# Norm passes moved from VectorE to GpSimd, and urgent work put first, in a two-layer attention and MLP kernel

## The chip, the cores and the metric

The kernel runs on one core of a Trainium2 chip. A core has TensorE (PE, matrix products), VectorE (DVE), ScalarE (ACT, here mostly exponentials), GpSimd (POOL) and SyncE (SP, which only starts transfers). They run side by side and wait for one another by semaphores. The metric is device time in microseconds (us) from the first to the last instruction; lower is better. "Faster" or "slower" by over 2% is told apart from "the same".

## The reference

Two layers, each an attention block A and an MLP block B, over 2048 tokens of width 512. Attention has 32 heads of width 16 that share one set of keys and values. B mixes shifted tokens and then applies an MLP of width 1792. The norms have no learned factors.

```python
def _layernorm(x):  return (x - mean(x)) / sqrt(var(x) + 1e-5)

def _A_ref(x, wq, wk, wv, wo):                 # x: 1 x 2048 x 512
    q = (x @ wq) as 32 heads of 16;  k = x @ wk;  v = x @ wv     # k, v: one head for all
    p = softmax(q k^T * 16**-0.5)              # 32 x 2048 x 2048
    return (p v) @ wo

def _B_ref(x, w1, w2, w3, w4):
    h = gelu(layernorm(x) @ w1)
    g = the four quarters of h, shifted by +1, -1, +2, -2 tokens
    x1 = x + g @ w2
    return x1 + gelu(layernorm(x1) @ w3) @ w4

x = x + _A_ref(layernorm(x));  x = x + _B_ref(layernorm(x))      # layer 0
x = x + _A_ref(layernorm(x));  x = x + _B_ref(layernorm(x))      # layer 1
```

Two facts shape the kernel. 32 x 2048 x 2048 exponentials per layer have to be made. And layer 1's attention needs keys of all tokens, so it cannot finish a query before layer 0 has finished its last token.

## The kernel before

The Python program builds a list of operations with durations it assumes, and runs a list scheduler over them (class `Plan`). The order that comes out is the instruction order of each engine; semaphores guard the data. So a changed duration, engine or priority changes the order of everything after it. Tokens come in tiles of 128, grouped in chunks: 4 x 4 tiles in layer 0, and 4, 4, 4, 2, 2 tiles in layer 1. While one chunk's attention runs, the dense work of the chunk before it (output projection, mixer, MLP) fills TensorE.

**Exponentials.** Most of them go through ScalarE, two score banks of 512 columns at a time (`declare_unit`). Seven EA buffers hold the results until the value product (PV) has read them:

```python
o = q.feeds = op("ACT", lambda e: e.activation(self.EA[:, ea, :, :], self.PB[:, b0:b0 + 2, :], ACTF.Exp,
                                               scale=0.25), writes=bk + [("EA", ea)], ...)     # L994
```

The others are made as a "pair" on VectorE and GpSimd (`declare_pair`): VectorE turns scores into 16-bit integers J (L1015), which are bit patterns of powers of two; two shifted copies JK (L1025) are made on GpSimd, or on VectorE if four are outstanding there; three value products with weighted values VD add them up. The pair is given out (`assign`) only if banks are free and if VectorE has little side work ready:

```python
if self.pl.backlog() > y or ...:  return False         # y = 1 (us) in most chunks
```

**Priorities.** Small numbers go first: 0 for scores of ScalarE's units, 2 for value products, 10 for dense work (`URGE`: 1.0 for the last chunk of layer 0). One rule lets dense work follow dense work, ahead of all else, to save a switch on TensorE:

```python
if stick and o.prio > 2 and o.pe[0] == self.pe_kind and not any(... > x for x in due):
    key = (self.STICK, o.seq)                          # STICK = -1
```

When TensorE has done little for a while, the plan inserts products of ones by zeros (`filler`: ONES, NIL) that keep its clock up.

**Norms.** Each norm has statistics (`stats`, L723 and L725), the power -0.5 (`rstd`, on GpSimd, L745) and one pass per tile (`apply`, L752). In the mixer there are two norms in a row: block B's input is itself a norm, and B begins with a norm; the second factor follows from the first variance, so one pass more per tile (L1289) does it:

```python
def apply(self, out, src, tb, tags, writes, dur, prio):
    self.pl.op("DVE", lambda e: e.tensor_scalar(out=out, in0=src, scalar1=self.MV[:, tb, 0:1],
               scalar2=self.SM[:, 0, tb:tb + 1], op0=ALU.subtract, op1=ALU.mult), ...)            # L752
...
# mixer_in: Y = norm(X); ZR = norm(Y)
for tb in tiles:
    self.apply(self.Y[:, tb % 6, :], self.X32[:, tb, :], tb, ...)
    op("DVE", lambda e, tb=tb: e.tensor_scalar(out=self.ZR[:, tb % 4, :], in0=self.Y[:, tb % 6, :],
               scalar1=self.SM[:, 1, tb:tb + 1], scalar2=0.0, op0=ALU.mult, op1=ALU.add), ...)    # L1289
```

The rows ZR (four tiles) are transposed on TensorE (L769), copied back (L776) and fed to the products with W1 or W3. The same four slots of ZR serve the mixer's second norm, the MLP's norm, and the input norms of both layers (`ln_in`; in layer 1 its rows give the keys and values of layer 1).

**The end of a block.** When all keys of a block of heads are done, `block_end` copies the sum (ACCF), makes reciprocals of the row sums and scales (OS, OT) at priority 5; after the eighth block the chunk's output projection and the rest follow (`chunk_end`).

Of the kernel before, what the change touches and what calls it, by code (L numbers as in the profile page):

```python
# [31 lines left out]
class Plan:  # L32
# [29 lines left out]
    SPARE = 0  # L62

    def __init__(self, nc, pool_banks):
        self.nc = nc
        self.res = {}
        self.ops = []
        self.now = 0.0
        self.free_at = {e: 0.0 for e in ENGINES}
        self.heap = {e: [] for e in ENGINES}  # L70
        self.order = {e: [] for e in ENGINES}
        self.events = [0.0]
        self.pool = [(0.0, b) for b in pool_banks]
        self.pool_last = {}
        self.left = 0
        self.dma_free = 0.0
        self.pe_kind = None
        self.pe_end = 0.0
        self.lane = [0.0] * 4
        self.port = 0.0  # L80
        self.window = 0
        self.activity = [0.0]
        self.warm = False
        self.release = 0.0
        self.entry = 0.0
        self.pace = None
        self.filler = None
        self.debt = 0.0
        self.debt_at = 0.0
        self.base = 10.0  # L90
        self.units = []
        self.attach = None
        self.loose = False
# [97 lines left out]
    def _pick(self, eng, t, dense=False):  # L191
        h = self.heap[eng]
        if dense:
# [6 lines left out]
            and self.pe_kind == "P"  # L200
        due = list(limit) + self.due(h, t) if stick else ()
        best = None
        bank = None
        for o in h:
            if o.ready > t + 1e-9:
                continue
# [12 lines left out]
            if stick and o.prio > 2 and o.pe[0] == self.pe_kind and not any(self.run_end(o, t) + self.SWITCH > x for x in due):  # L219
                key = (self.STICK, o.seq)  # L220
            if best is not None and key > best[0]:
                continue
# [269 lines left out]
EPS = 1e-5  # L492
# [3 lines left out]
class Kernel:  # L496
# [4 lines left out]
    URGE = ((10, 10, 10, 1.0), (10, 10, 10, 1.5, 10))  # L501
    SPILLED = 7
    SHIFTS = (1, -1, 2, -2)
# [47 lines left out]
    def memory(self):  # L551
# [32 lines left out]
        self.EA = sb("EA", [self.N_EA, 2, 512])  # L584
        self.J = sb("J", [self.N_J, 1024], dt.uint16)
# [134 lines left out]
    def stats(self, src, tiles, tagf, prio):  # L720
        op = self.pl.op
        for tb in tiles:
            op("DVE", lambda e, tb=tb: e.bn_stats(self.ST6[:, tb, :], src(tb)),  # L723
               reads=[tagf(tb)], writes=[("ST", tb)], dur=0.606, prio=prio)
            op("DVE", lambda e, tb=tb: e.bn_aggr(self.MV[:, tb, :], self.ST6[:, tb, :]),  # L725
               reads=[("ST", tb)], writes=[("MV", tb)], dur=0.09, prio=prio)

    def rstd(self, tiles, prio, both=False):
        op = self.pl.op
        a, b = tiles[0], tiles[-1] + 1  # L730
        mv = self.MV[:, a:b, 1]
        k = 2 if both else 1

        def tg(name):
            return [(name, t) for t in tiles]
        var, aux = self.SM[:, 2, a:b], self.SM[:, 3, a:b]
        op("DVE", lambda e: e.tensor_scalar(out=var, in0=mv, scalar1=EPS, scalar2=None, op0=ALU.add),  # L737
           reads=tg("MV"), writes=tg("S2"), dur=0.08, prio=prio, port=True)
        if both:
            op("DVE", lambda e: e.reciprocal(aux, var), reads=tg("S2"), writes=tg("S3"), dur=0.1, prio=prio)  # L740
            op("DVE", lambda e: e.tensor_tensor(out=aux, in0=aux, in1=mv, op=ALU.mult),
               reads=tg("MV"), writes=tg("S3"), dur=0.08, prio=prio, port=True)
            op("DVE", lambda e: e.tensor_scalar(out=aux, in0=aux, scalar1=EPS, scalar2=None, op0=ALU.add),
               writes=tg("S3"), dur=0.08, prio=prio, port=True)
        op("POOL", lambda e: e.tensor_tensor(out=self.SM[:, 0:k, a:b], in0=self.SM[:, 2:2 + k, a:b],  # L745
                                             in1=self.MH[:, 0:k, a:b], op=ALU.pow),
           reads=tg("S2") + (tg("S3") if both else []) + [("MH",)], writes=tg("R1") + (tg("R2") if both else []),
           dur=0.3 + 0.2 * (b - a) * k, prio=self.QUICK if prio is None else prio)

    def apply(self, out, src, tb, tags, writes, dur, prio):  # L750

        self.pl.op("DVE", lambda e: e.tensor_scalar(  # L752
            out=out, in0=src, scalar1=self.MV[:, tb, 0:1], scalar2=self.SM[:, 0, tb:tb + 1],
            op0=ALU.subtract, op1=ALU.mult),
            reads=tags + [("MV", tb), ("R1", tb)], writes=writes, dur=dur, prio=prio, port=True)

    def transpose(self, tiles, dst, dtags, prio):

        op = self.pl.op
        n = len(tiles)  # L760
        for hd in range(2):
            L = Late()
            for j in range(2):
                dc = 2 * hd + j

                def fpe(e, dc=dc, j=j, L=L):
                    ins = None
                    for i, tb in enumerate(tiles):
                        ins = e.transpose(self.PBH[:, L.bank, j * 512 + i * 128:j * 512 + (i + 1) * 128],  # L769
                                          self.ZR[:, tb % 4, dc * 128:(dc + 1) * 128], self.IDENT)  # L770
                    return ins
                op("PE", fpe, reads=[("ZR", tb % 4) for tb in tiles] + [("ID",)], writes=[L],
# [8 lines left out]
    def ln_in(self, la, tiles, prio=None):  # L781
# [5 lines left out]
        self.rstd(tiles, prio)  # L787
        for tb in tiles:
            self.apply(self.ZR[:, tb % 4, :], src(tb), tb, [("X", tb)], [("ZR", tb % 4)],
                       0.456 if la else 0.355, prio)  # L790
# [3 lines left out]
                       [[("YT", slot, hd, t % 4) for t in tiles] for hd in range(2)], prio)  # L794
# [286 lines left out]
    def block_end(self, la, c, b, end):  # L1081
# [22 lines left out]
        else:  # L1104
            self.last_copy = op("DVE", lambda e: e.tensor_copy(acc, self.PB[:, self.ACC, 0:n]),
               writes=[("AC",), ("ACCF", m)], dur=t_ps(n), prio=0, side=False)
        L = Late()
# [7 lines left out]
        op("PE", fz, reads=[("ACCF", m), ("SELC",)], writes=[L], pe=("F", 60 * nq, 4 * nq), prio=5, take=L)  # L1115
# [4 lines left out]
        op("DVE", frec, writes=[L, ("RZ", m)], dur=0.17, prio=5, give=L)  # L1120
        M = Late()
        for h in range(nq // 2):
# [8 lines left out]
            op("PE", fx, reads=[("RZ", m), ("ID",)], writes=[M], pe=("P", 256, 256, range(4)), prio=5,  # L1131
# [3 lines left out]
           reads=[("ACCF", m)], writes=[M, ("OS", m)], dur=t_ps(n), prio=5, give=M)  # L1135
        r0 = 64 * (b % 2)
        hw = n // 2
        if c == len(self.CHUNKS[la]) - 1 and b >= self.LATE_OT:
            N = Late()

            def fo(e):
# [9 lines left out]
               pe=("P", 2 * hw, hw, (r0 // 32, r0 // 32 + 1)), prio=5, take=N)  # L1151
            op("DVE", lambda e: e.tensor_copy(self.OT[r0:r0 + 64, b // 2, 0:n], self.PB[r0:r0 + 64, N.bank, 0:n]),
               writes=[N, ("OT", b)], dur=t_ps(n), prio=5, give=N)
        else:
# [4 lines left out]
               reads=[("OS", m)], writes=[("OT", b)], dma=128 * n, parts=8, prio=5)  # L1159
# [9 lines left out]
    def pump(self, now):  # L1169
# [3 lines left out]
        while True:  # L1173
            if sum(1 for o in self.units[-4:] if not (o.placed and o.end <= now + 1e-9)) >= 3:
                break
            while self.hi in self.given:
                self.hi += 1
            if self.hi >= n:
                break
# [103 lines left out]
    def mixer_in(self, la, c, tiles, tail, more=None):  # L1283
# [3 lines left out]
        for tb in tiles:  # L1287
            self.apply(self.Y[:, tb % 6, :], self.X32[:, tb, :], tb, [("X", tb)], [("Y", tb % 6)], 0.456, None)
            op("DVE", lambda e, tb=tb: e.tensor_scalar(  # L1289
# [3 lines left out]
               dur=0.265, port=True)  # L1293
# [71 lines left out]
    def mlp(self, la, tiles, tail, defer=False):  # L1365
# [14 lines left out]
        for f in range(14):  # L1380
# [10 lines left out]
            if tail:  # L1391
                op("ACT", lambda e, f=f, L=L: e.activation(self.G2[:, f, 0:n], self.PB[:, L.bank, 0:n],
                                                           ACTF.Gelu_apprx_tanh),
                   writes=[L, ("G2", f)], dur=0.0505 + n / 1200, give=L)
# [18 lines left out]
        self.mlp_out(la, tiles)  # L1413

    def mlp_out(self, la, tiles):
        op = self.pl.op
        g2 = [("G2", f) for f in range(14)]
        for i, tb in enumerate(tiles):
            L = Late()
            for h in range(7):  # L1420
                def fpe(e, h=h, i=i, tb=tb, L=L):
                    ins = None
                    for f in (2 * h, 2 * h + 1):
                        ins = self.dot(e, L.bank, 512, self.G2[:, f, i * 128:(i + 1) * 128], self.W4[:, f, :],
# [50 lines left out]
```

## Time and profile before

| | before |
|---|---|
| device time, median of 3 runs | 1617.7 us (1616.78 to 1618.05) |
| span of the profiled run | 1615.1 us |
| exponentials on ScalarE (1024 columns, mean) | 1504, 1105 ns |
| conversions to J on VectorE (512 columns) | 1088, so 544 pairs |
| shifts JK on GpSimd / on VectorE | 983 (1054 ns) / 105 (702 ns) |
| norm passes on VectorE | 32 Y<-X 934 ns, 32 ZR<-Y 733 ns, 16 + 16 ZR<-X 904 and 524 ns, 32 second passes 539 ns |
| start of steady exponentials / end of the last | 43.8 us / 1549.3 us |
| mean granted TensorE clock | 0.999 |

How to read the lines: L12 is a line of the kernel's program; `out<-in` names the tiles; `x` is a count. In a group the numbers after the bar are busy us and mean ns of one, then the idle time of that engine just before, and what released it. Waits are "who waited for whom: total us, times, longest us". Timeline lines are start us, length us, engine, line, operation and count, with the idle time before in brackets. The busy time of one instruction on ScalarE overlaps the next: steady exponentials follow each other every 0.917 us (246 in 225.69 us). W3, W4, W1, W2 and WO products all stand under L612, and `W` in a tile's name is one of the weights, `G` the MLP's inner values, `GP` the mixer's, `ZT` transposed norm rows.

### The profile page before, as it was taken

To read this page: it belongs to the slowest core of one execution; us is meant where nothing else is said; L and a number is where in the kernel's file an instruction comes from. 1 tells how busy PE (TensorE), PEld (TensorE's weight loads), DVE (VectorE), ACT (ScalarE), POOL (GpSimd) and SP (SyncE) were. 2 spreads that over 40 slices of the span, in tenths; PEclk is the share of its full clock that TensorE was granted. 3 is DMA by queue.
4 is the path that set the end of the run, shared out by engine and by line. 5 is a ranking of instruction groups with operands and counts; after the bars stand their busy time and mean duration, and the time that the engine had idled before them with its cause. 6 is when DMAs were issued, how large, how long until landed. Compare 5 with 4: busy or idle time off the path is not lost.

```text
span 1615.1 us, 63788 instructions
## 1 busy us (share of the span) xinstructions
PE 1567.6 (97%) x28953; PEld 654.9 (41%) x28953; DVE 1245.5 (77%) x2222; ACT 1500.5 (93%) x1580; POOL 1118.4 (69%) x1083
## 2 busy tenths in 40 slices
PE   8999999999999999999999999999999999999999
PEld 3333333434333333333333434333343334544555
DVE  8777887778887679887776678878678885778863
ACT  4999999999999999999998499999999998999952
POOL 4798877866787766776673477677777867768631
PEclk9999999999999999999999999999999999999999
DMA  6100010001000001000000000100000000000000
GB/s 207 17 6 5 7 18 6 6 4 17 7 6 4 6 4 19 6 4 2 2 2 2 3 9 9 19 4 5 9 18 5 6 5 15 16 8 7 6 17 19
DMA packets 32144, 21.55 MB, mean 13 GB/s; under 512 B 12672, under 2 KB 31360, under 8 KB 31872
## 3 DMA queue, kind: packets, MB, share of 16 engines
q1 hardware_dynamic: 31872, 17.47, 4.5%
q8 instruction: 226, 3.70, 1.0%
q14 instruction: 46, 0.38, 0.1%
HBM read 7.90 MB, written 2.10 MB: 6 GB/s over the span
## 4 chain that ended last, share of the span: by engine, by line
ACT 64%; PE 33%; DVE 2%; issue 0%; DMA 0%; POOL 0%; SPq 0%; POOLq 0%
ACT EA L994 59%; PE PB L612 12%; PE PB L950 10%; PE PB L1073 8%; ACT G L1403 2%; PE PB L769 1%; ACT L994 1%; ACT GP L1323 1%; ACT L1403 1%; ACT L1323 0%; DVE ZR L752 0%; DVE ST L723 0%; DMA X<-in_A_x_dram 0%; DVE J L1015 0%; PE PB L878 0%
## 5 line engine op out<-in xcount | busy, mean ns | idle before, releaser
L994 ACT ACTIVATE EA<-PB 128x1024 bf16<-128x1024 f32 x1504 | 1390.6, 1105 | 66.6 <-PE PB L1073 33.8
L1025 POOL TENSOR_SCALAR JK<-J 128x1024 uint16<-128x1024 uint16 x983 | 1035.6, 1054 | 402.4 <-DVE J L1015 257.4
L1015 DVE TENSOR_SCALAR J<-PB 128x512 uint16<-128x512 f32 x1088 | 702.4, 683 | 185.1 <-PE PB L950 181.1
L950 PE MATMUL PB<-QT,KT 32*128 32x512 bf16 (+1 forms) x4608 | 624.4, 359 | 30.5 <-ACT EA L994 18.6
L1073 PE MATMUL PB<-EA,VP 128*32 128x256 bf16 (+1 forms) x6784 | 388.4, 265 | 0.5
L950 PEld LDWEIGHTS PB<-QT,KT 32*128 32x128 bf16 x4608 | 161.3, 91 | 448.0 <-ACT EA L994 351.4
L1073 PE MATMUL PB<-JK,VD 128*32 128x256 bf16 (+1 forms) x4864 | 291.3, 265 | 2.9 <-POOL JK L1025 1.9
L1073 PEld LDWEIGHTS PB<-EA,VP 128*32 128x32 bf16 x6784 | 157.1, 95 | 175.3 <-issue 149.6
L612 PE MATMUL PB<-ONES,NIL 128*32 128x512 bf16 x1984 | 177.1, 387 | 7.4 <-DVE ZR L752 2.8
L1073 PEld LDWEIGHTS PB<-JK,VD 128*32 128x32 bf16 x4864 | 114.9, 95 | 128.0 <-issue 78.8
L612 PE MATMUL PB<-ZT,W 128*32 128x512 bf16 (+2 forms) x2816 | 166.6, 341 | 0.0
L1073 PE MATMUL PB<-J,VD 128*32 128x256 bf16 (+1 forms) x2432 | 154.9, 264 | 1.3 <-DVE J L1015 0.8
L612 PE MATMUL PB<-W,G 128*32 128x512 bf16 x1792 | 122.9, 380 | 0.3 <-DVE X L1279 0.3
L1396 DVE CAST G<-PB 128x512 bf16<-128x512 f32 (+2 forms) x126 | 72.3, 582 | 34.7 <-PE PB L612 33.4
L612 PEld LDWEIGHTS PB<-ZT,W 128*32 128x32 bf16 x2816 | 67.7, 96 | 26.1 <-issue 13.0
L1025 DVE TENSOR_SCALAR JK<-J 128x1024 uint16<-128x1024 uint16 x105 | 73.2, 702 | 2.9 <-PE PB L1073 1.9
L1073 PEld LDWEIGHTS PB<-J,VD 128*32 128x32 bf16 x2432 | 60.6, 95 | 35.4 <-issue 21.6
L612 PEld LDWEIGHTS PB<-ONES,NIL 128*32 128x32 bf16 x1984 | 49.6, 96 | 42.4 <-issue 11.2
L745 POOL TENSOR_TENSOR SM<-SM,MH 128x4 f32<-128x4 f32 (+4 forms) x30 | 31.7, 1058 | 40.8 <-DVE SM L737 24.8
L1133 DVE TENSOR_TENSOR OS<-ACCF,PB 128x512 bf16<-128x512 bf16 (+1 forms) x72 | 44.6, 622 | 17.7 <-PE PB L1127 17.3
L612 PEld LDWEIGHTS PB<-W,G 128*32 128x32 bf16 x1792 | 42.2, 96 | 31.8 <-issue 11.7
L1403 ACT ACTIVATE G<-G 128x3584 bf16<-128x3584 bf16 (+2 forms) x18 | 46.0, 2601 | 9.4 <-DVE G L1396 9.3
(88 smaller groups left out, 861.5 us busy)
## 6 DMA issues: line engine op xcount, KB each, us to landing
OT<-OS SPq DMA_DIRECT2D x424, 8.0 KB, 1.8
W<-in_B_w_dram SPq DMA_DIRECT2D x2, 1792.0 KB, 14.4
QT<-QS SPq DMA_DIRECT2D x40, 64.0 KB, 2.4
X<-in_A_x_dram SPq DMA_DIRECT2D x8, 256.0 KB, 5.4
out_dram<-OUTB SPq DMA_DIRECT2D x16, 128.0 KB, 1.7
OT<-OS SPq DMA_DIRECT2D x104, 4.0 KB, 1.7
W<-in_B_w_dram SPq DMA_DIRECT2D x2, 512.0 KB, 8.4
WQ<-in_A_wq_dram SPq DMA_DIRECT2D x1, 512.0 KB, 5.0
```

The lines of the kernel that those rows point to most:

```text
L612: ins = e.matmul(self.PB[32 * g:32 * g + 32, bank, 0:n], lhsT=lhsT[:, 32 * g:32 * g + 32], rhs=rhs, start=start, stop=stop, tile_position= ...
L745: op("POOL", lambda e: e.tensor_tensor(out=self.SM[:, 0:k, a:b], in0=self.SM[:, 2:2 + k, a:b], in1=self.MH[:, 0:k, a:b], op=ALU.pow), read ...
L769: ins = e.transpose(self.PBH[:, L.bank, j * 512 + i * 128:j * 512 + (i + 1) * 128], self.ZR[:, tb % 4, dc * 128:(dc + 1) * 128], self.IDENT)
L950: ins = e.matmul(self.PB[:, bank, j * n:(j + 1) * n], lhsT=self.KT[32 * h:32 * h + 32, la, (kb + j) * 128:(kb + j + 1) * 128], rhs=self.QT ...
L994: o = q.feeds = op("ACT", lambda e: e.activation(self.EA[:, ea, :, :], self.PB[:, b0:b0 + 2, :], ACTF.Exp, scale=0.25), writes=bk + [("EA" ...
L1015: o = op("DVE", lambda e, i=i, L=L: e.tensor_scalar(out=J[:, i * 512:(i + 1) * 512], in0=self.PB[:, L.bank, :], scalar1=128 * LOG2E * 0.25 ...
L1025: x = op(eng, lambda e, k=k, r=r: e.tensor_scalar(out=self.JK[:, r, :], in0=J, scalar1=float(self.STEPS[k]), scalar2=1.0, op0=ALU.add, op1 ...
L1073: ins = e.matmul(self.PB[32 * x:32 * x + 32, self.ACC, p * hw:p * hw + hw], lhsT=v[:, la, kb + j, :], rhs=ap[:, i, j * w + u * hw:j * w + ...
L1133: op("DVE", lambda e: e.tensor_tensor(out=self.OS[:, m, 0:n], in0=acc, in1=self.PB[:, M.bank, 0:n], op=ALU.mult), reads=[("ACCF", m)], wri ...
L1323: return e.activation(self.GP[:, par, :, 2:2 + n], self.GP[:, par, :, 2:2 + n], ACTF.Gelu_apprx_tanh)
L1396: op("DVE", lambda e, f=f, L=L: e.tensor_copy(self.G2[:, f, 0:n], self.PB[:, L.bank, 0:n]), writes=[L, ("G2", f)], dur=t_ps(n), give=L)
L1403: ins = e.activation(self.G2[:, a:a + 7, 0:n], self.G2[:, a:a + 7, 0:n], ACTF.Gelu_apprx_tanh)
```

## The change

It moves the norm passes and most small statistics to GpSimd (not those at the start of layer 0), raises the priority of the aggregation of statistics on VectorE, and splits the two powers into two instructions, so that the first norm need not wait for the second's factor. Layer 1's input norm gets rows of its own: QS, which otherwise holds query projections. Value products that one of the next three exponentials waits for go first (PINNED). The rule that dense work follows dense work is off while an urgent dense operation (priority up to 1.2) is ready, and near the end. In the last chunk of each layer the end of a block gets priority 1.0, and in the last chunk of layer 1 all that follows has it too. In the last chunk the MLP's gelu writes into the EA buffers, which are free by then, and not into G2, which the products before it still read.

```diff
+    PINNED = -2
+    RUSHED = 1.2
 ...
         stick = eng == "PE" and not dense and not joins and self.STICK is not None and t < self.pe_end + 0.05 \
-            and self.pe_kind == "P"
+            and self.pe_kind == "P" \
+            and not any((0 < o.prio <= self.RUSHED if o.side else self.closing) and o.ready <= t + 1e-9 for o in h)
+        pinned = {p for u in self.units[-3:] if not u.placed for p in u.preds
+                  if p.eng == "PE" and p.prio == 2 and not p.placed} if eng == "PE" and not dense else ()
 ...
+            if eng == "ACT" and self.closing and o.side and not all(u.placed for u in self.units[-4:]):
+                continue
 ...
+            if o in pinned:
+                key = (self.PINNED, o.seq)
 ...
-    URGE = ((10, 10, 10, 1.0), (10, 10, 10, 1.5, 10))
+    URGE = ((10, 10, 10, 1.0), (10, 10, 10, 1.5, 1.0))
+    RUSH = ((10, 10, 10, 1.0), (10, 10, 10, 5, 1.0))
+    CLOSING = 12
 ...
+        self.G2E = self.EA.rearrange("p a b c -> p (a b) c")
 ...   # stats
-               reads=[("ST", tb)], writes=[("MV", tb)], dur=0.09, prio=prio)
+               reads=[("ST", tb)], writes=[("MV", tb)], dur=0.09, prio=self.QUICK if prio is None else prio)
 ...   # rstd: var + eps, power, and for both norms the second factor
+        eng = "DVE" if early else "POOL"
+        def power(out, src, tags, r):
+            op("POOL", lambda e: e.tensor_tensor(out=out, in0=src, in1=self.MH[:, 0, a:b], op=ALU.pow),
+               reads=tags + [("MH",)], writes=tg(r), dur=0.3 + 0.2 * (b - a), prio=prio)
-        op("DVE", lambda e: e.tensor_scalar(out=var, in0=mv, scalar1=EPS, scalar2=None, op0=ALU.add),
+        op(eng, lambda e: e.tensor_scalar(out=var, in0=mv, scalar1=EPS, scalar2=None, op0=ALU.add),
            reads=tg("MV"), writes=tg("S2"), dur=0.08, prio=prio, port=True)
+        power(one, var, tg("S2"), "R1")
         if both:
-            op("DVE", lambda e: e.reciprocal(aux, var), ...)
-            op("DVE", ... aux * mv);  op("DVE", ... aux + EPS)
+            op(eng, lambda e: e.tensor_tensor(out=aux, in0=one, in1=one, op=ALU.mult), ...)
+            op(eng, ... aux * mv);  op(eng, ... aux + EPS)
+            power(two, aux, tg("S3"), "R2")
-        op("POOL", ... both powers in one tensor_tensor)
 ...   # apply
-        self.pl.op("DVE", lambda e: e.tensor_scalar(
+        early = prio is not None
+        self.pl.op("DVE" if early else "POOL", lambda e: e.tensor_scalar(
 ...
-            reads=tags + [("MV", tb), ("R1", tb)], writes=writes, dur=dur, prio=prio, port=True)
+            reads=tags + [("MV", tb), ("R1", tb)], writes=writes, dur=dur if early else 0.65, prio=prio if early else self.QUICK, port=True)
 ...   # ln_in
+        base = (self.QS, "QS") if la else (self.ZR, "ZR")
         for tb in tiles:
-            self.apply(self.ZR[:, tb % 4, :], src(tb), tb, [("X", tb)], [("ZR", tb % 4)],
+            self.apply(base[0][:, tb % 4, :], src(tb), tb, [("X", tb)], [(base[1], tb % 4)],
 ...   # block_end: all its side operations take prio=fin in place of 5
+        fin = min(5, self.RUSH[la][c])
 ...   # pump
+            self.pl.closing = self.hi + self.CLOSING >= n
 ...   # mixer_in, second pass
-            op("DVE", lambda e, tb=tb: e.tensor_scalar(
+            op("POOL", lambda e, tb=tb: e.tensor_scalar(
 ...
-               dur=0.265, port=True)
+               dur=0.65, prio=self.QUICK, port=True)
 ...   # mlp and mlp_out, last chunk
-                op("ACT", lambda e, f=f, L=L: e.activation(self.G2[:, f, 0:n], self.PB[:, L.bank, 0:n],
+                op("ACT", lambda e, f=f, L=L: e.activation(self.G2E[:, f, 0:n], self.PB[:, L.bank, 0:n],
                                                            ACTF.Gelu_apprx_tanh),
-                   writes=[L, ("G2", f)], dur=0.0505 + n / 1200, give=L)
+                   writes=[L, ("EA", f // 2)], dur=0.0505 + n / 1200, give=L)
```

## What was predicted

> **What bounds the kernel now.** I read the totals of the page first, then the chain that ended last, then ScalarE's waits and its timeline at each gap, and last the other engines' timelines at those moments.
>
> The page's busy totals, and its chain by engine:
>
> ```profile
> PE 1567.6 (97%) x28953; PEld 654.9 (41%) x28953; DVE 1245.5 (77%) x2222; ACT 1500.5 (93%) x1580; POOL 1118.4 (69%) x1083
> ...
> ACT 64%; PE 33%; DVE 2%; issue 0%; DMA 0%; POOL 0%; SPq 0%; POOLq 0%
> ```
>
> ScalarE and TensorE are both close to full. TensorE's 97% holds 1984 matmuls of ones by zeros (`ONES,NIL`), which keep its clock up. The timeline shows 112 dense matmuls in 6.22 us, so four side by side take 0.222 us, and 1984/4 x 0.222 = 110 us of TensorE is spare in the whole run. VectorE and GpSimd have a quarter of their time free, and the chain gives them 2% and 0%: a change of their load alone cannot be worth its own size. ScalarE's waits (total us, times, longest us):
>
> ```profile
> ACT EA L994 <- PE PB L1073: 33.8, 18, 10.2
> ACT EA L994 <- PE PB L950: 31.8, 12, 18.3
> ACT GP L1312 <- PE PB L612: 14.0, 1, 14.0
> ACT G L1392 <- PE PB L612: 11.1, 14, 6.5
> ACT G L1403 <- DVE G L1396: 9.3, 1, 9.3
> ```
>
> Row 1: an exponential waits for the value product (L1073) that still reads the EA buffer it is to write. Row 2: it waits for scores; 21.8 us of it lie in the first 80 us, which this change leaves alone, and 8.4 us at 930 us, where layer 1 waits for its last keys. Rows 3 to 5 are the end, after the last exponential (1549.3 us). The longest wait of row 1 in ScalarE's and TensorE's timelines:
>
> ```profile
> 898.57 1.02 ACT L994 ACTIVATE EA<-PB 128x1024 bf16<-128x1024 f32 x1 [10.15 <-PE PB L1073]
> 889.11 4.93 PE L612 MATMUL PB<-W,G 128*32 128x512 bf16 x88
> 893.87 1.05 PE L612 MATMUL PB<-ZT,W 128*32 128x256 bf16 x32
> 895.07 1.48 PE L612 MATMUL PB<-ZT,W 128*32 128x256 bf16 x48
> ```
>
> TensorE is not idle there. It runs 10 us of dense MLP products while the value product that would free EA stands ready: the plan's STICK rule lets dense work follow dense work. The same shape is at 1369 us (5.2 us) and 1181 us (3.1 us). By stretch, row 1 has 20.9 us between 855 and 931, and 10.6 us between 1100 and 1400.
>
> The second norm at the end of layer 0, in VectorE's timeline:
>
> ```profile
> 767.36 3.35 DVE L752 TENSOR_SCALAR Y<-X,MV,SM 128x512 bf16<-128x512 f32 x4
> 784.82 0.34 DVE L1289 TENSOR_SCALAR ZR<-Y,SM 128x512 bf16<-128x512 bf16 x1
> 812.09 1.12 DVE L1289 TENSOR_SCALAR ZR<-Y,SM 128x512 bf16<-128x512 bf16 x3 [1.33 <-PE PB L769]
> ```
>
> The mixer's second norm writes the four row slots of ZR. The first norm (Y) is done at 770.7, but ZR is filled only at 813.2: one slot at 785, the other three when layer 1's input norm of the chunk before (L752, ZR<-X, until 807) and its transposes (until 811) are done with the same slots. So 42 us of the path to layer 1's last keys are a buffer wait. I found it by asking why work that was ready at 771 came at 812.
>
> **What the Trainium skill says.** (1) "SBUF — State Buffer", Who interferes with whom: a `tensor_scalar` of VectorE in a two-port mode and a GpSimd instruction exclude each other for the whole instruction. The trace agrees (min/median/max ns):
>
> ```profile
> L752 DVE TENSOR_SCALAR Y<-X,MV,SM x32: 529/1048/1403, 230.8 to 1560.5; 128x512 bf16<-128x512 f32 x32
> L1289 DVE TENSOR_SCALAR ZR<-Y,SM x32: 256/346/1134, 233.0 to 1561.9; 128x512 bf16<-128x512 bf16 x32
> ```
>
> The same instruction takes 529 ns or over 1 us; the surplus is up to half a microsecond and more, which fits a wait for a GpSimd shift of 1054 ns. (2) "GPSIMD Engine Reference", Engine selection: one-input elementwise work is about as fast on GpSimd as one element a cycle, two-input work some 2x slower. The trace agrees: the 1024-element shift (one input) took 1054 ns, the 512-element add of Y and X (two inputs) 1169 ns. (3) "Perfetto Trace Analysis", Optimizing Scalar/DVE Operations: moving work between these two might not help, since they share a port; no run shows this yet. (4) The same page, Identifying the Most-Contended Engine: matmul busy time is a bad measure of headroom. It agrees: 177.1 us of the busy sum are the ones-by-zeros matmuls.
>
> **The change, part by part.**
>
> *Norm passes to GpSimd.* Off VectorE go, by the groups of lines: 28.9 (32 Y<-X) + 23.0 (32 ZR<-Y) + 14.0 (16 ZR<-X of layer 1) + 16.8 (32 second scalings) = 82.7 us, with some 15 us of small statistics (the means and variances proper stay, and their last step now goes first on VectorE). On GpSimd, half of a 1054 ns shift is 0.53 us, and the plan is told 0.65, so I take 0.6: 112 x 0.6 = 67 us. Nine second powers add about 9 x 0.4 us (two of 1.02 us in place of one of 1.64), and 26 + 27 small operations about 0.15 us each = 8 us. GpSimd goes from 1118 to some 1197 us (74%) and does not become the bound. What VectorE gains buys something in one way only: the plan hands a pair of exponentials to VectorE and GpSimd only when no more than 1 us of side work stands ready on VectorE. The nine mixer groups, ten MLP groups and seven input norms hold it by their passes for something like 30 to 45 us (half of the 82.7, the rest being port waits). At 36 to 38 pairs per 100 us (75 shifts in 400 to 500) that is 11 to 17 pairs; some are lost as GpSimd's bursts push shifts back to VectorE. I take 7 pairs more, each an exponential of 0.917 us less on ScalarE (225.69 us for 246): **-6 us**.
>
> *Urgent value products (PINNED).* A value product that one of the next exponentials waits for goes ahead of all. The 10.6 us at 1181 and 1369 vanish; the displaced dense products move into stretches where TensorE runs ones by zeros (152 of them in 1400 to 1500, 38 fours, 8.4 us). Most of it is gained: **-8 us**. The 20.9 us at 855 to 931 count with the boundary.
>
> *Boundary (own rows in QS, RUSH, urgency over STICK).* The 42 us buffer wait goes, so W1, gelu, mixing, W3 and W4 of layer 0's last chunk start earlier. Yet ScalarE loses only 20.9 + 8.4 = 29.3 us there, and TensorE has little room: from 750 to 1055 it ran 28 + 220 + 160 ones-by-zeros matmuls, 102 fours x 0.222 = 22.6 us, and was idle some 5. So at most 27 us can be pressed out, and that only with perfect packing. GpSimd's passes lengthen the last norm before the keys: now four take 1.92 us (924.41), then 4 x 0.6 = 2.4. I take somewhat under half: **-12 us**.
>
> *Tail (URGE and RUSH 1.0 for the last chunk, CLOSING, gelu into EA).* From 1549.3 to the end TensorE is almost solid with W3 and W4 of the last two chunks; only what is not dense can go:
>
> ```profile
> L612 PE MATMUL PB<-ONES,NIL 128*32 128x512 bf16 x116 | 9.5, 384 | 2.2 <-DVE MV L725 0.7 <-DVE ZR L752 0.7 <-DVE OS L1133 0.5
> ```
>
> 116/4 x 0.222 = 6.4 us plus 2.2 idle = 8.6. With the last chunk first, the chunk before fills its waits; GpSimd's slower norms (three passes 1.8 instead of 1.06 us, the mixer's chain about 1 us longer) then lie beside dense work. **-6 us**.
>
> Sum: -6 - 8 - 12 - 6 = -32 us. The parts overlap, since they draw on the same spare TensorE time (110 us, much of it where ScalarE is the limit and nothing dense is left). I take off 3 us: 1617.7 - 29 = about **1589 us**.
>
> **The rivals.**
>
> *A: TensorE takes the place of the waits.* At 855 to 922 it is solid, so freeing EA only delays the dense products, and the wait comes back as one for keys (row 2 of the waits). For it: 10 us of PE at 100% in 889 to 899. Against it: the 42 us buffer wait and the ones-by-zeros on either side. The boundary then gives 3 us in place of 12: about 1600.
>
> *B: GpSimd becomes late.* Mixer norms become a row of about 2.8 us of statistics and 8 passes, 7.6 us in one engine, ahead of shifts, and the shifts then hold pairs and banks. For it: GpSimd waits for VectorE's J in 257.4 us, so its work arrives in clumps. Against it: 402.4 us idle before the shifts. It would cost some 10 to 20 pairs, 10 to 18 us: about 1605, and with A about 1615.
>
> *C: all of it adds up.* Boundary 22, row 1 gone elsewhere 10, tail 8, pairs 15: 55 us, about 1563. Against it: both main engines would have to be full at once.
>
> **Range and chances.** The middle is 1589. A and half of B give the upper end, 1611; two thirds of C's surplus give the lower, 1570. Two per cent is 1585.3, just under my middle: faster by over 2% 0.43, within 2% 0.54, slower by over 2% 0.03, since no part adds work to ScalarE or TensorE.
>
> **What would show it.** Right: row 1 of ScalarE's waits under 8 us; the second norm's rows within 10 us of the first's; ScalarE's waits between 850 and 935 under 15 us; ones-by-zeros in the last 65 us under 60; exponentials on ScalarE near 1497; norm passes on GpSimd 0.55 to 0.7 us. Wrong: row 2 grown by what row 1 lost (A); shifts on VectorE well over 105 and fewer pairs than 544 (B); norm passes over 0.9 us. I would be most wrong if the count of pairs moved by tens, for each is worth almost 1 us and I have it only from a rule on backlog.

## The result, and the profile after

The change made the kernel slower: 1754.26 us (1751.06 to 1755.56) against 1617.24 us, a ratio of 1.0842 with a 95% interval of 1.0827 to 1.0858. Line numbers are those of each kernel's own program: in the changed one exponentials are L1018, scores L974, value products L1097, norm passes L774 and L1315, transposes L792 and their copies L799. The page's totals, chain and clock row of the changed kernel:

```profile
PE 1607.2 (92%) x28733; PEld 665.0 (38%) x28733; DVE 1189.5 (68%) x2105; ACT 1509.1 (86%) x1576; POOL 1288.4 (73%) x1225
...
PEclk9999989989889988899989999899998999988999
...
ACT 41%; PE 37%; POOL 15%; DVE 4%; issue 2%; DMA 0%; POOLq 0%; SPq 0%
```

The clock row before:

```profile
PEclk9999999999999999999999999999999999999999
```

ScalarE has about the same work (1509 us, before 1500) but a smaller share of a longer span. GpSimd, 0% of the chain before, now holds 15%, and TensorE's clock, 9 tenths or more in every slice before, dips below that again and again. ScalarE's and TensorE's waits of the changed kernel (who for whom: total us, times, longest us):

```profile
ACT EA L1018 <- PE PB L974: 145.1, 87, 18.4
ACT G L1429 <- DVE G L1422: 34.2, 3, 15.8
ACT EA L1018 <- PE PB L1097: 27.1, 4, 12.0
```

```profile
PE PB L792 <- POOL ZR L1315: 45.4, 8, 6.7
PE PB L792 <- POOL ZR L774: 32.3, 8, 5.6
PE PB L1097 <- POOL JK L1049: 20.1, 13, 4.2
...
PE PB L792 <- POOL QS L774: 6.4, 2, 5.4
```

TensorE stands 84 us at transposes (L792) for norm rows from GpSimd; before it had no such wait. The groups of GpSimd say why:

```profile
L774 POOL TENSOR_SCALAR Y<-X,MV,SM 128x512 bf16<-128x512 f32 x32 | 67.0, 2095 | 0.0
L774 POOL TENSOR_SCALAR ZR<-Y,MV,SM 128x512 bf16<-128x512 bf16 x32 | 66.3, 2082 | 1.1
L774 POOL TENSOR_SCALAR QS<-X,MV,SM 128x512 bf16<-128x512 f32 x16 | 33.1, 2081 | 0.7
L1315 POOL TENSOR_SCALAR ZR<-Y,SM 128x512 bf16<-128x512 bf16 x32 | 21.6, 696 | 0.2
```

The pass (x - mean) * rstd takes 2.08 to 2.10 us where the plan was told 0.65. The second pass, one factor and + 0, takes 0.696. One mixer group in the timeline, all engines:

```profile
232.95 2.08 POOL L774 TENSOR_SCALAR Y<-X,MV,SM 128x512 bf16<-128x512 f32 x1
235.01 2.70 POOL L1315 TENSOR_SCALAR ZR<-Y,SM 128x512 bf16<-128x512 bf16 x4
237.76 0.61 PE L792 MATMUL PB<-IDENT,ZR 128*128 128x128 bf16 x4 [5.93 <-POOL ZR L1315]
238.96 1.02 ACT L1018 ACTIVATE EA<-PB 128x1024 bf16<-128x1024 f32 x1 [6.17 <-PE PB L974]
239.49 0.69 DVE L799 COPY ZT<-PB 128x1024 bf16<-128x1024 bf16 x1 [12.14 <-PE PB L792]
```

The transposes sit in TensorE's fixed order where the plan thought the rows would be ready. They are not, so TensorE stands 5.93 us, which is about what the plan was wrong by over the four tiles (4 x 1.43 + 4 x 0.05 = 5.9 us); the score products queued behind do not start, and ScalarE and VectorE run dry 6 and 12 us. And it goes on after the rows have come. Stretches of the same place (us busy and instructions of PE, PEld, DVE, ACT and POOL, then the granted clock):

```profile
229.00:233.00 4.00, 2.48 (x30) 0.64 (x30) 0.00 (x0) 3.78 (x5) 4.00 (x5) 1.00 0.03 6
233.00:236.00 3.00, 0.00 (x0) 0.00 (x0) 0.00 (x0) 0.00 (x0) 3.00 (x3) 0.76 0.00 0
236.00:239.00 3.00, 1.24 (x8) 0.61 (x9) 0.00 (x0) 0.04 (x1) 2.83 (x5) 0.50 0.02 5
243.00:247.00 4.00, 4.00 (x41) 1.12 (x38) 3.27 (x6) 2.61 (x3) 0.67 (x1) 0.50 0.00 0
251.00:255.00 4.00, 4.00 (x74) 1.65 (x71) 2.59 (x4) 3.38 (x4) 0.69 (x1) 0.92 0.01 4
```

The clock halves during the stand and is at 0.50 until about 251, so ScalarE has gaps of 0.3 to 0.7 us between exponentials. "TensorE: Matmul & The Clock Gate", What's actually happening, in the Trainium skill gives two clock states, full and half, set by recent activity; this trace agrees on the two states (1.00 and 0.50, mixed only within a stretch). What brings the full one back it does not show: from 243 to 247 TensorE is busy for 4.00 of 4.00 us and still at 0.50. From 40 us on, by stretches of 10 us (2 x (1 - clock) x length), TensorE spent 189 us at half clock; before, none.

### The profile page after: what moved, and what is told of

Read it like the earlier page. It is cut to its first block, busy times and chain, and to the rows that moved or that the text cites. A ratio compares the mean times of both kernels' runs of the same rounds, so it can differ in the third digit from the quotient of the medians.

```text
span 1753.8 us, 63432 instructions
## 1 busy us (share of the span) xinstructions
PE 1607.2 (92%) x28733; PEld 665.0 (38%) x28733; DVE 1189.5 (68%) x2105; ACT 1509.1 (86%) x1576; POOL 1288.4 (73%) x1225
## 4 chain that ended last, share of the span: by engine, by line
ACT 41%; PE 37%; POOL 15%; DVE 4%; issue 2%; DMA 0%; POOLq 0%; SPq 0%
ACT EA L1018 37%; PE PB L974 12%; PE PB L625 12%; PE PB L1097 10%; POOL Y L774 4%; POOL JK L1049 4%; POOL ZR L774 3%; PE PB L792 2%; POOL QS L774 2%; DVE J L1039 2%; ACT G L1429 2%; POOL SM L756 1%; POOL ZR L1315 1%; ACT L1018 1%; ACT GP L1349 1%
## 5 line engine op out<-in xcount | busy, mean ns | idle before, releaser
L1018 ACT ACTIVATE EA<-PB 128x1024 bf16<-128x1024 f32 x1500 | 1399.8, 1079 | 173.8 <-PE PB L974 145.1
L1049 POOL TENSOR_SCALAR JK<-J 128x1024 uint16<-128x1024 uint16 x951 | 1001.8, 1053 | 373.5 <-DVE J L1039 215.9
L974 PE MATMUL PB<-QT,KT 32*128 32x512 bf16 (+1 forms) x4608 | 637.8, 369 | 25.5 <-ACT EA L1018 15.9
L1097 PE MATMUL PB<-EA,VP 128*32 128x256 bf16 (+1 forms) x6764 | 388.8, 269 | 1.3 <-DVE ACCF L1129 0.5
L974 PEld LDWEIGHTS PB<-QT,KT 32*128 32x128 bf16 x4608 | 160.5, 91 | 447.8 <-ACT EA L1018 306.0
L1097 PE MATMUL PB<-JK,VD 128*32 128x256 bf16 (+1 forms) x4904 | 298.6, 272 | 20.8 <-POOL JK L1049 20.1
L1097 PEld LDWEIGHTS PB<-EA,VP 128*32 128x32 bf16 x6764 | 159.4, 96 | 163.9 <-issue 132.9
L1097 PEld LDWEIGHTS PB<-JK,VD 128*32 128x32 bf16 x4904 | 116.8, 96 | 162.8 <-issue 87.7
L1097 PE MATMUL PB<-J,VD 128*32 128x256 bf16 (+1 forms) x2452 | 158.1, 267 | 2.0 <-DVE J L1039 1.2
L625 PE MATMUL PB<-ONES,NIL 128*32 128x512 bf16 x1724 | 153.9, 395 | 6.4 <-DVE ZR L774 2.2
L792 PE MATMUL PB<-IDENT,ZR 128*128 128x128 bf16 x320 | 37.6, 285 | 77.8 <-POOL ZR L1315 45.4
L1049 DVE TENSOR_SCALAR JK<-J 128x1024 uint16<-128x1024 uint16 x145 | 99.3, 694 | 14.2 <-PE PB L1097 12.7
L799 DVE COPY ZT<-PB 128x1024 bf16<-128x1024 bf16 (+2 forms) x38 | 22.7, 602 | 123.3 <-PE PB L792 123.1
L1097 PEld LDWEIGHTS PB<-J,VD 128*32 128x32 bf16 x2452 | 60.9, 96 | 44.6 <-issue 26.4
L774 POOL TENSOR_SCALAR ZR<-Y,MV,SM 128x512 bf16<-128x512 bf16 x32 | 66.3, 2082 | 1.1
L774 POOL TENSOR_SCALAR Y<-X,MV,SM 128x512 bf16<-128x512 f32 x32 | 67.0, 2095 | 0.0
```

The lines of the kernel that those rows point to most:

```text
L625: ins = e.matmul(self.PB[32 * g:32 * g + 32, bank, 0:n], lhsT=lhsT[:, 32 * g:32 * g + 32], rhs=rhs, start=start, stop=stop, tile_position= ...
L774: self.pl.op("DVE" if early else "POOL", lambda e: e.tensor_scalar(out=out, in0=src, scalar1=self.MV[:, tb, 0:1], scalar2=self.SM[:, 0, tb ...
L799: return e.tensor_copy(dst[:, 2 * hd:2 * hd + 2, 0:n * 128], self.shaped(self.PBH[:, L.bank, :], [2, 512])[:, :, 0:n * 128])
L974: ins = e.matmul(self.PB[:, bank, j * n:(j + 1) * n], lhsT=self.KT[32 * h:32 * h + 32, la, (kb + j) * 128:(kb + j + 1) * 128], rhs=self.QT ...
L1049: x = op(eng, lambda e, k=k, r=r: e.tensor_scalar(out=self.JK[:, r, :], in0=J, scalar1=float(self.STEPS[k]), scalar2=1.0, op0=ALU.add, op1 ...
L1097: ins = e.matmul(self.PB[32 * x:32 * x + 32, self.ACC, p * hw:p * hw + hw], lhsT=v[:, la, kb + j, :], rhs=ap[:, i, j * w + u * hw:j * w + ...
```

## The experiments

The theory (P) is that the slow pass on GpSimd, and the plan's ignorance of it, is all of the loss. The rival (O) is that the new rules of order broke up dense work.

**The pass by itself.** This kernel leaves out norms and attention and runs single forms on GpSimd, each six times:

```diff
+        def ts(e, o, i, s1, s2, a, b):
+            return e.tensor_scalar(out=o, in0=i, scalar1=s1, scalar2=s2, op0=a, op1=b) if b is not None else \
 ...
+            lambda e: ts(e, T["SMpp"], XF, PM, PR, S, M),
+            lambda e: ts(e, T["SMii"], XF, 0.25, 1.5, S, M),
 ...
+            lambda e: ts(e, T["AMpp"], XF, PM, PR, A, M),
+            lambda e: ts(e, T["M1p"], XF, PR, None, M, None),
```

A form's name gives its operations in order (S subtract, M multiply, A add, 1 no second one), then its scalars (p a pointer: one value for each row, read from a tile; i an immediate: a constant in the instruction). A B at the end is bf16 input.

> This kernel leaves the whole computation out and only runs single tensor_scalar forms on GpSimd, 128x512, one after the other with nothing beside them. In the changed kernel the pass (x - mean) * rstd with two pointer scalars took 2.08 us and the second pass (x * factor + 0) 0.696 us. Theory F (the form is slow: subtract first, or two pointers): the form alone takes 2.0 to 2.1 us here too, and at least one form that can do the same work, multiply then add or subtract, takes 0.5 to 0.8 us. Rival C (contention with VectorE made it slow): the same form takes 0.6 to 0.8 us when VectorE is silent. Rival T (the f32 input or the bf16 output is slow): the bf16 input takes a different time from the f32 input.

Groups of this kernel (the form is in the tile's name after T; after the bar, busy us and mean ns):

```profile
L29 POOL TENSOR_SCALAR TSMpp<-XF,PM,PR 128x512 bf16<-128x512 f32 x6 | 12.5, 2077 | 7.5 <-DVE Z L56 7.0
L29 POOL TENSOR_SCALAR TMSpp<-XF,PR,PM 128x512 bf16<-128x512 f32 x6 | 12.5, 2077 | 0.6
L29 POOL TENSOR_SCALAR TSMppB<-XB,PM,PR 128x512 bf16<-128x512 bf16 x6 | 12.5, 2076 | 0.6
L29 POOL TENSOR_SCALAR TSMii<-XF 128x512 bf16<-128x512 f32 x6 | 11.5, 1924 | 0.5
L30 POOL TENSOR_SCALAR TM1p<-XF,PR 128x512 bf16<-128x512 f32 x6 | 9.4, 1564 | 0.6
L29 POOL TENSOR_SCALAR TAMpp<-XF,PM,PR 128x512 bf16<-128x512 f32 x6 | 4.6, 770 | 0.6
L29 POOL TENSOR_SCALAR TMAii<-XF 128x512 bf16<-128x512 f32 x6 | 3.7, 620 | 0.5
L29 DVE TENSOR_SCALAR TDVpp<-XF,PM,PR 128x512 bf16<-128x512 f32 x6 | 3.3, 546 | 135.9 <-POOL UO L29 135.7
```

Theory F holds: 2077 ns with VectorE silent, so it is neither contention nor the type (2076 with bf16 input). Nor is it the pointers: with immediates it still takes 1924. It is the operations: subtract and multiply in either order. Add then multiply does the same work with a negated mean in 770 ns; VectorE takes 546 ns for subtract then multiply and for multiply then add. Why GpSimd is slow at the one and not at the other, no run shows.

**Norms back on VectorE, the rest kept.**

```diff
-        self.pl.op("DVE" if early else "POOL", ...)          # apply, second pass, small statistics
+        self.pl.op("DVE", ...)                               # as before; all priorities, QS and gelu into EA kept
```

> The changed kernel with the norm passes and their small statistics put back on VectorE as before; all priorities, the own rows and the gelu buffer stay changed. Theory P (the passes on GpSimd cost it all): 1580 to 1605 us, TensorE clock back to 0.99 or more, ScalarE's waits for scores after 80 us under 20 us. Rival O (the new order is bad, dense work is broken up): over 1680 us, as slow as the changed kernel less some 30 us.

1604.59 us, ratio 0.9916 (0.9900 to 0.9933): P, at the top of its range, and 75 us below O's. Its page and ScalarE's waits:

```profile
PE 1557.5 (97%) x28829; PEld 651.5 (41%) x28829; DVE 1241.9 (78%) x2226; ACT 1501.5 (94%) x1582; POOL 1102.9 (69%) x1063
```

```profile
ACT EA L1009 <- PE PB L965: 38.4, 16, 17.7
ACT G L1420 <- DVE G L1413: 29.1, 3, 18.1
ACT EA L1009 <- PE PB L1088: 4.6, 2, 3.2
```

So the passes on GpSimd, with the small statistics that moved along, cost 1754.3 - 1604.6 = 150 us of the changed kernel.

**The plan told the truth.** Same work on the same engines; one number altered.

```diff
-            ... dur=dur if early else 0.65, ...
+            ... dur=dur if early else 2.08, ...
```

> The changed kernel with one number altered: the scheduler is told 2.08 us for the first passes on GpSimd in place of 0.65. The work on every engine stays the same. Theory D (the wrong duration put the transposes too early in TensorE's order, and TensorE stood at them): TensorE's waits for norm rows fall from 84 us to under 15 us, the clock is 0.99 or more, and the time is 1600 to 1640 us, since GpSimd still holds 166 us of passes and takes fewer shifts. Rival G (GpSimd has no room for 166 us of passes whatever the order): the time stays over 1680 us with shifts late.

1667.87 us, ratio 1.0307 (1.0288 to 1.0325); the clock is back at 0.996. TensorE's waits for norm rows:

```profile
PE PB L792 <- POOL ZR L774: 3.2, 2, 3.0
PE PB L792 <- POOL ZR L1315: 3.1, 4, 1.8
```

The stands are gone, and with them 86 us of the 150. The time misses D's range by 28 us and stays under G's 1680: the plan's error is more than half of the loss, and the passes cost something when it is told the truth, too. ScalarE shows where: against the version with norms on VectorE, its waits rise from 82.1 to 127.8 us in total (value products 4.6 to 56.2), and it makes 1524 exponentials in place of 1508, since there are 524 pairs in place of 540. The wait for value products:

```profile
ACT EA L1018 <- PE PB L1097: 56.2, 13, 11.5
```

45.7 + 16 x 0.917 = 60 of the 63 us between the two. GpSimd makes 892 shifts in place of 963: slow passes crowd them out in this order too.

**Half told.**

```diff
+            ... dur=dur if early else 1.36, ...
```

> The changed kernel with the plan told 1.36 us for the subtract-first pass, half way between 0.65 (told in the change: 1754 us) and the true 2.08 (1668 us). Theory D (the loss grows with the error of the plan, as TensorE stands at the transposes for the difference): TensorE's waits for norm rows 25 to 50 us, between the 84 and the 6 us of the two, clock 0.96 to 0.98, and 1695 to 1730 us. Rival: the time has nothing to do with what the plan is told and falls outside that range, under 1668 or over 1754 us.

1734.92 us, ratio 1.0718 (1.0688 to 1.0748), 5 us over the range, clock 0.953. TensorE's waits for norm rows:

```profile
PE PB L792 <- POOL ZR L1315: 20.1, 7, 4.4
PE PB L792 <- POOL ZR L774: 15.2, 8, 4.1
...
PE PB L792 <- POOL QS L774: 4.9, 3, 2.7
```

The waits fell as expected, to 40 us, the time by less: half the error leaves 67 of the 86 us. The half clock hardly fell either, from 189 to 164 us.

**Only the norms moved, nothing else.**

```diff
+   # the kernel before, with rstd, apply and the second pass of the change
```

> The kernel before with only the norm passes and small statistics moved to GpSimd, at the assumed 0.65 us; no new priorities, no own rows, no gelu buffer. Theory P: 1730 to 1790 us, clock 0.93 to 0.95, TensorE waits 70 us or more for norm rows. Rival O: 1610 to 1640 us.

1815.44 us, ratio 1.1219 (1.1197 to 1.1242), 25 us over P's range and far from O's, with clock 0.938 and 92.5 us of TensorE's waits for norm rows:

```profile
PE PB L778 <- POOL ZR L761: 49.6, 11, 5.5
PE PB L778 <- POOL ZR L1298: 42.9, 8, 6.4
```

So the new rules did not make the loss: without them it is 61 us larger.

**The stands filled.** Half clock or standing still? TensorE gets work in the stands, and all else is as in the changed kernel.

```diff
+   if prio is None and n > 2 and hd == 0 and j == 0:          # before the wait for norm rows
+       o.pre = lambda e, L=L: [self.dot(e, L.bank, 512, self.NIL, self.ONES, True, True) for _ in range(20)]
```

> The changed kernel with 20 fours of ones-by-zeros (20 x 0.222 = 4.4 us) put into TensorE's stream just before it waits for norm rows, in groups of three or four tiles; the plan, its order and GpSimd's work are the same. TensorE now works through most of each stand instead of idling, and the rows come no earlier. If the half clock that follows each stand is the larger part of the 86 us that the wrong order costs (1754 against 1668 us): clock 0.98 or more and 1670 to 1705 us. If the stand itself is the larger part: the clock recovers and the time stays at 1715 to 1755 us.

1733.62 us, ratio 1.0718 (1.0700 to 1.0735); half clock fell from 189 to 65 us, TensorE's waits for norm rows from 84 to 18 us. At the place shown above the clock is whole again once the rows are there, and ScalarE steadies at once:

```profile
229.00:233.00 4.00, 3.91 (x42) 1.24 (x46) 0.00 (x0) 3.56 (x4) 4.00 (x5) 0.67 0.03 8
233.00:236.00 3.00, 3.00 (x56) 1.31 (x48) 0.00 (x0) 0.00 (x0) 3.00 (x3) 0.87 0.00 0
243.00:247.00 4.00, 4.00 (x63) 1.34 (x65) 3.41 (x6) 3.97 (x5) 2.25 (x2) 1.00 0.00 0
```

Yet only 21 us came back, though two thirds of the half clock are gone: by the ranges set before, the stand itself is the larger part. The share of the clock is at least 21 us, and more by what the filling overshoots in the shorter stands (estimate: 320 fours x 0.222 = 71 us were put in where 66 us of stands went) and by the third of the half clock that is left. The half-told plan, though its order is another one, points the other way: there the stands halved, the half clock stayed and little time came back. How the 86 us divide between the two stays open.

**The fast form.** Theory F as a repair: (x + (-mean)) * rstd on GpSimd.

```diff
+   op("POOL", lambda e: e.tensor_scalar(out=self.NM[:, a:b], in0=self.MV[:, a:b, 0], scalar1=-1.0, scalar2=0.0, op0=ALU.mult, op1=ALU.add), ...)
-   scalar1=self.MV[:, tb, 0:1], ... op0=ALU.subtract, op1=ALU.mult
+   scalar1=self.NM[:, tb:tb + 1], ... op0=ALU.add, op1=ALU.mult          # told 0.65, or 0.78
```

> The changed kernel with the pass on GpSimd written as (x + (-mean)) * rstd in place of (x - mean) * rstd, for which one small GpSimd operation per group makes -mean; same engine, same order rules, the plan still told 0.65 us. Measured alone the add-first form took 0.770 us, the subtract-first form 2.077. Theory F (the form alone made the change slow): first passes 0.75 to 0.85 us, TensorE's waits for norm rows under 15 us, clock 0.99 or more, 1585 to 1610 us. Rival E (norms on GpSimd are bad in whatever form, since its shifts wait behind them): 1640 us or more.

> The same with the plan told 0.78 us for the pass in place of 0.65. Theory D (what counts is that the plan is near the truth; an error of 0.13 us is small): within 10 us of the run with 0.65, TensorE's waits for norm rows a few us lower. Rival: an error of four times 0.13 us a group already costs, and this is over 15 us faster.

Told 0.65: 1639.41 us, ratio 1.0142 (1.0124 to 1.0161), outside both ranges. Told 0.78: 1613.79 us, ratio 0.9975 (0.9966 to 0.9984). First passes take 0.77 to 0.80 us in both. TensorE's waits for norm rows, first told 0.65, then 0.78:

```profile
PE PB L802 <- POOL ZR L1325: 7.9, 9, 2.6
...
PE PB L802 <- POOL ZR L779: 1.6, 2, 1.4
```

```profile
PE PB L802 <- POOL ZR L1325: 1.3, 3, 0.8
```

The form takes back 115 to 140 of the 150 us. Told truly, this is the whole change as it was meant, and it is worth 0.25%, not the 29 us I forecast; with the norms on VectorE it is 9 us better still. Since the small statistics are on GpSimd in this version too, they are no large part of the 150 us. 25 us between the two are more than D allowed for 0.13 us, and more than the 8 us of stands explain; they lie in the rival's range, but a mere shift of the order, measured below, can move as much.

> The kernel before with only the norm passes and small statistics on GpSimd, in the add-first form, the plan told 0.78 us; no new priorities, no own rows. The same with the subtract form and 0.65 took 1815 us. My prediction's part for this: -6 us, so 1605 to 1617 us with some 551 pairs. Rival B (GpSimd's bursts cost pairs and lengthen the chains): 1622 to 1650 us with fewer than 544 pairs.

The fast form alone on the kernel before (told 0.78) gave 1635.05 us, ratio 1.0108 (1.0086 to 1.0130): rival B's range in time, but not by its loss of pairs, for there are the 551 that I had forecast. ScalarE's waits for value products and scores are 81.2 us in place of 65.6, which is most of the 17 us.

**Single rules on the kernel before, and the plan's own scatter.**

```diff
+   if o in pinned: key = (self.PINNED, o.seq)                          # PINNED alone
+   base = (self.QS, "QS") if la else (self.ZR, "ZR")                   # own rows alone
-               reads=[("Y", tb % 6)], writes=[("X", tb)], dur=1.3, port=True)
+               reads=[("Y", tb % 6)], writes=[("X", tb)], dur=1.17, port=True)   # add of Y and X, alone
```

> The kernel before with only the PINNED rule (a value product that one of the next exponentials waits for goes first). My prediction's part: -8 us and something at the boundary, so 1603 to 1611 us, ScalarE's waits for value products under 8 us. Rival A (the wait comes back as one for scores and keys): 1612 us or more, with the waits for scores grown by what those for value products lost.

> The kernel before with only the own rows QS for layer 1's input norm; norms on VectorE, no new priorities. My prediction's boundary part rests on this: the 42 us wait for ZR between the first and the second norm at the end of layer 0 goes. If the path to layer 1's last keys was held by it: the second norm's rows come within 10 us of the first's, and the time is 1603 to 1612 us. Rival A (TensorE is full there, so nothing comes of it): the rows come early all the same and the time stays at 1613 to 1622 us.

> The kernel before with one assumed duration set to its true value: the add of Y and X on GpSimd is told 1.17 us (measured 1.169) in place of 1.3. No work is added, taken away or moved to another engine; only the order the plan finds may shift. If small order shifts are worth little: 1614 to 1621 us. If the plan's order alone moves the time by a per cent: outside 1608 to 1627 us, and differences of 10 us between the versions above are not to be read as the worth of a single rule.

PINNED alone: 1628.54 us, ratio 1.0063 (1.0047 to 1.0080). ScalarE's waits:

```profile
ACT EA L999 <- PE PB L955: 50.6, 19, 17.7
...
ACT EA L999 <- PE PB L1078: 6.4, 5, 2.1
```

The wait for value products fell from 33.8 to 6.4 as I said, and the wait for scores rose from 31.8 to 50.6: rival A took back most of it.

Own rows alone: 1631.89 us, ratio 1.0087 (1.0072 to 1.0102). VectorE's timeline at the end of layer 0:

```profile
777.94 2.41 DVE L752 TENSOR_SCALAR Y<-X,MV,SM 128x512 bf16<-128x512 f32 x2
780.27 2.24 DVE L1291 TENSOR_SCALAR ZR<-Y,SM 128x512 bf16<-128x512 bf16 x2
785.47 0.61 DVE L1291 TENSOR_SCALAR ZR<-Y,SM 128x512 bf16<-128x512 bf16 x2
```

The second norm's rows now end at 786 in place of 813, and the time is 15 us worse, above both ranges. So that buffer wait did not hold the time. Why it is worse, and not the same as A has it, no run shows.

One assumed duration set to its true value, with no other edit: 1638.67 us, ratio 1.0130 (1.0113 to 1.0147), outside 1608 to 1627. This is a warning for all of the above: a harmless edit, and one towards the truth, shifts the order of the rest and moved this kernel by 21 us. So 11 or 15 us for a single rule is not its worth, and the 150, 86 and 63 us above are not good to the last 20.

> The version with the norms back on VectorE (1604.6 us), now without the PINNED rule; the rest of the change stays. PINNED alone on the kernel before gave 1628.5 us, 11 us more. If it is bad in itself: 1590 to 1600 us. If it is needed beside the other rules (urgent dense work no longer follows itself only): 1606 to 1620 us, with ScalarE's waits for value products back to some 20 us or more.

> The best version so far (norms back on VectorE, rest of the change kept, 1604.6 us) with the assumed duration of the add of Y and X set from 1.3 to its true 1.17 us, as in the run that shifted the kernel before by 21 us. If the gain of 13 us belongs to the new rules: 1600 to 1612 us. If it belongs to one lucky order of the plan: 1613 us or more, inside the spread that the kernel before showed (1617 to 1639).

Norms on VectorE without PINNED: 1620.53 us, ratio 1.0023 (1.0016 to 1.0030), waits for value products back at 27.5 us. The same version with PINNED and the 1.17 us edit: 1611.42 us, ratio 0.9967 (0.9954 to 0.9980). The first is half a us over the range of "needed beside the other rules", the second inside the range that gives the gain to the rules. The fairest reading compares like with like, where only the rules differ:

| norms, and what the plan is told | without the rules | with them | gain |
|---|---|---|---|
| VectorE, as before | 1617.6 us | 1604.6 us | 13 us |
| VectorE, add of Y and X 1.17 us | 1638.7 us | 1611.4 us | 27 us |
| GpSimd, fast form, 0.78 us | 1635.1 us | 1613.8 us | 21 us |
| GpSimd, slow form, 0.65 us | 1815.4 us | 1754.3 us | 61 us |

The sign is the same four times. Where TensorE does not stand, the rules together gave 13 to 27 us; three orders are few for more than that.

## Why the prediction was wrong

**Norm passes to GpSimd: the step that failed.** "On GpSimd, half of a 1054 ns shift is 0.53 us, and the plan is told 0.65, so I take 0.6: 112 x 0.6 = 67 us." It measured 67.0 + 66.3 + 33.1 + 21.6 = 188 us. I took one form's rate (add, then multiply) for another's (subtract, then multiply) and read an assumed duration in the change as if it were measured. The Trainium skill's rule that I used ("GPSIMD Engine Reference", Engine selection: one-input work at about one element a cycle) fits multiply-add (620 ns for 512 elements, 1.2 ns each with all overhead) and fails for this form: (2077 - 1222)/256 = 3.3 ns an element, from 512 and 256 elements. The measurement decides. The same row recommends VectorE for adding and multiplying, which I passed over. I had named "norm passes over 0.9 us" as what would show me wrong.

**"No part adds work to ScalarE or TensorE", hence 0.03 for slower.** True and beside the point. In a kernel whose order is fixed by assumed durations, an underestimate on a side engine becomes a stand on the main one. 86 of the 150 us are that, half clock included; 63 us stay when the plan knows the slow pass.

**GpSimd does not become the bound.** As a share it did not (73%). But the wait for it, which I had left out, came to bind: 15% of the chain in place of 0%.

**Pairs, -6 us.** 548 against 544, in place of my 551. With the fast form alone there were just 551, and the kernel was 17 us slower than before all the same: the count was right, but the step from pairs to time failed, since the waits grew by more.

**PINNED, -8 us.** The waits between 1100 and 1400 went from 10.6 to some 3 us once the norms were on VectorE (1050 to 1500: 1.6 + 1.4), as I had it, and taking the rule out of that version cost 16 us. Alone it did nothing good.

**Boundary, -12 us.** I read the 42 us buffer wait as part of the path to layer 1's last keys. It did go (in the changed kernel the second norm's rows directly follow the first's, at 863.6), but with the norms on VectorE ScalarE still waits 15.1 + 3.2 us there for scores and value products and 11.0 more at a gelu (770 to 950 us), 29.3 in all; before, it was 32.3 in that stretch. About the 3 us that I gave rival A are what came.

**Tail, -6 us.** With norms on VectorE the last exponential ends at 1539.4 and the run at 1602.4: 63.0 us of tail in place of 65.8, so -3; the ones-by-zeros in it fell from 116 to 72, not to nothing.

Of the rules I expected -26 us in sum; the like pairs give -13, -27 and -21. Of the passes on GpSimd I expected -6. Even in the fast form and told truly they cost 9 us beside the rules and 17 without them, both inside the scatter of the order, and the kernel comes to 1613.8 us, still above my upper end of 1611. So the slow form made the large loss, but a true 0.77 us would not have made the forecast come true either.

## What to carry to other kernels

Before moving an elementwise pass to GpSimd, measure that very pair of operations there by itself; write it as multiply and add (in either order) if it can be so written, and compare with VectorE's time. In a kernel whose order comes from assumed durations, compare each assumed duration with the trace first: an engine that works in a fixed order can stand for the whole error (5.9 us in the group shown; 84 us of 80 x 1.43 = 114 over this run), and what is queued behind it stands too. A truer number is no promise of a better order, though: 1.17 in place of 1.3 was 21 us slower. So find out how much a harmless edit moves such a kernel before a difference of 1% is read as the worth of a rule.

## What was not expected of the hardware

On GpSimd a pass with one operation is slower than one with two: subtract or multiply alone took 1.56 us for 128x512, multiply and then add 0.62 to 0.77 us. With subtract in either place, first or after multiply, the two operations took 2.08 us with two pointers. VectorE took 546 ns for each of the two forms tried there.
